# Fused attention and two FFNs in one planned program: other lead times and a later-transfer assumption in the planner, constants by one GpSimd transfer, twelve early vector operations on GpSimd

## The chip, the cores and the metric

The kernel runs on one core of one Trainium2 chip. The metric is the device time of one execution in microseconds (us); the time quoted is the median of three runs. "Before" is the kernel as it stood, 839.82 us.

## The reference, cut to what matters

```python
def _attn_ref(q, k, v):                 # q, k, v: [4, 8, 576, 64]
    scores = (1 / sqrt(64)) * q @ k^T
    mask = (rel >= 0) & (rel < 64)      # rel = query position - key position
    scores = where(mask, scores, -1e9)
    attn = exp(scores - max)
    attn = attn / (sum(attn) + 1e-9)
    return attn @ v

x = attention as [2304 tokens, 512]
x = square(relu(x @ moe_w_in)) @ moe_w_out        # 512 -> 2048 -> 512
out = leaky_relu(x @ moe2_w_in, 0.01) @ moe2_w_out
```

The FFN weights arrive as 64-bit floats and are turned into 32-bit words on the chip.

## The kernel before, in words

The 2304 tokens are cut into 18 blocks of 128. Attention is windowed, so a block of queries sees 192 keys. Each block has two quads of four heads. A quad is: scores on PE (`scores`, L495), mask with scale on DVE (`mask`, L516, one operand in PSUM, the other the mask tile), row maximum on DVE (L530), four exponentials on ACT (L533), sum and reciprocal on DVE (L541, L542), normalisation on DVE (`norm` in `softmax`, L545, two operands in SBUF), transpose on PE against an identity tile (L565), copy on ACT, product with v on PE (`weigh`, L574), and a split of the result into a rounded part (ACT, L366) and a remainder (DVE, L369). The split serves all large products: each is done as three fp32r products, high by high, high by low and low by high.

A weight chunk of w_in or w_out of the first FFN (`weight`, L425) is loaded as 64-bit words (L390, three buffers `wst`), rebiased on ACT (L399), put together by three DVE operations (L402, L408, L414), cast on ACT (L366) and given its remainder on DVE (L369). Of the second FFN the weights are converted to DRAM (`weight_to_dram`, L442) while earlier stages run, and read back later.

In order of time the stages are: the first quads (blocks 0 and 1, then 2 to 5), the first FFN's units on tokens 0 to 767 (L730, `unit`; chunks j, and token parts A of 256, BB of 256, AB of 512 and C of 256), its second products (L742, `out_unit`), the third token group in plain steps while the remaining blocks of attention are computed, a "wide" stage for the last 1024 tokens with seven products for eight (L982, `wide_pair`), its second products (L742), then the second FFN with seven products for eight: first layer `pair` (L1104, from `x_combos` of the stored x and sums of weights) and second layer `superblock` (L1294).

What sets the order: nothing is ordered by hand. `build` records some thousand operations, each with engine, assumed cost, due time, reads, writes and buffers, into `Plan`. `Plan.order` (L164) then runs an event model with those costs: each engine takes the ready operation that is due first, a buffer is given out when its last user is done in the model, and a transfer takes an assumed issue time, start, rate and completion. The sequence that comes out is written into each engine's queue, in which the chip goes strictly in order. The table `PRM` (L46) holds the due times' lead values: `DS`, `SB`, `END` for the quads, `AL` and `CS` for the rebias and the DVE steps of a weight conversion, `EV0`, `EV1` for the evacuations at the end of a stage, `WP`, `W7` for the operand sums, `XS` for `x_combos`, `WI`, `WO2` for the stretch over which the second FFN's weights are converted. At the start, 40 products of zeros (`WARM`, L1420 to L1428) have the lowest priority of all: PE takes one whenever the model has nothing else ready for it. `NCOLD` of them are taken to be slower than the others.

The constants are three transfers at the start: a mask for pattern 1 on SP's queue (L509 called at L1430), a mask for pattern 0 (L1431) and the identity (L1432) on ACT's queue. Later pattern masks are loaded into the first tile's second half on SP's queue.

GpSimd (POOL) does nothing before but four memsets of constants.

Of the kernel before, what the change touches and what calls it, by code (L numbers as in the profile page):

```python
# [100 lines left out]
class Plan:  # L101
# [182 lines left out]
@with_exitstack  # L284
def attention_then_two_ffns(
    ctx: ExitStack,
    tc: tile.TileContext,
    qp: bass.AP,
    kp: bass.AP,
    vp: bass.AP,  # L290
    w1: list,
    w2: list,
    caps: bass.AP,
    ident: bass.AP,
    out: bass.AP,
):
    plan, _ = build(ctx, tc, qp, kp, vp, w1, w2, caps, ident, out)
# [8 lines left out]
def build(ctx, tc, qp, kp, vp, w1, w2, caps, ident, out, prm=PRM):  # L306
    nc = tc.nc
# [117 lines left out]
    def weight(k, c, gate=()):  # L425

        j, m = divmod(k, 2)
        cv = slot(ep, "e", [P, DM], I32, 4)
        w = slot(rings[f"w{m}"], f"w{m}", [P, 2, DM], F32R)
        wt[j, m] = w  # L430
        cs = prm["CS"]
        float_words(0, j, m, c, cv)
        op("act", act_cost(DM), c + 1.8 * cs, lambda: copy(w.ap[:, 0], f32(cv.ap)), [(cv, 0), *gate], [(w, 0)])
        op(
            "dve", dve_cost(DM), c + 2.5 * cs,
            lambda: sub(nc.vector, w.ap[:, 1], f32(cv.ap), w.ap[:, 0]),
            [(cv, 0), (w, 0)], [(w, 1)],
        )
# [66 lines left out]

    def load_cap(b, due, queue):

        dma(
            due, lambda: queue.dma_start(out=cap_s.ap[:, 1], in_=caps[:, pattern(b)]),  # L509
            P * P * 4, writes=[(cap_s, 1)],  # L510
        )

    def cap_of(b):
        return (cap_s, 1 if pattern(b) else 0)

    def mask(b, u, st):  # L516
        nc.vector.scalar_tensor_tensor(
            out=u.ap, in0=st.ap, scalar=SCALE,
            in1=cap_s.ap[:, cap_of(b)[1], :].unsqueeze(1).to_broadcast([P, HQ, P]),
            op0=ALU.mult, op1=ALU.min,  # L520
        )

    def softmax(u, dve_sum, due):

# [114 lines left out]
    def duo(b, e):  # L639

        if pattern(b):
            load_cap(b, e - prm["DS"] - 6.0, nc.sync)
# [27 lines left out]
        op("pe", 1.23, e - 1.8, run, rd, [(pv, 0)], margin=prm["SPARE"])  # L670
        to_x(b, pv, 0, KD, e - 0.6)
# [957 lines left out]
```

## Time and profile before

| | |
|---|---|
| runs | 839.82 us median (839.74 to 840.04) |
| profiled execution, its own time | 841.09 us |
| span of that execution, first to last instruction | 839.2 us |
| PE (matmul) | 819.8 us busy, 98% of the span |
| DVE | 584.1 us, 70% |
| ACT | 504.3 us, 60% |
| POOL | 0.2 us, 0% |

The profiled execution is 1.27 us above the median, and 1.89 us of its time lie outside the span. PE's share counts the products of zeros at the start and is a mean over all stages; which engine the others wait for changes from stage to stage, so the sections below go by stretches of the span.

### The profile page before, as it was taken

To read this page: it belongs to the slowest core of one execution; us is meant where nothing else is said; L and a number is where in the kernel's file an instruction comes from. 1 tells how busy PE (TensorE), PEld (TensorE's weight loads), DVE (VectorE), ACT (ScalarE), POOL (GpSimd) and SP (SyncE) were. 2 spreads that over 40 slices of the span, in tenths; PEclk is the share of its full clock that TensorE was granted. 3 is DMA by queue.
4 is the path that set the end of the run, shared out by engine and by line. 5 is a ranking of instruction groups with operands and counts; after the bars stand their busy time and mean duration, and the time that the engine had idled before them with its cause. 6 is when DMAs were issued, how large, how long until landed. Compare 5 with 4: busy or idle time off the path is not lost.

```text
span 839.2 us, 14312 instructions
## 1 busy us (share of the span) xinstructions
PE 819.8 (98%) x5312; PEld 739.6 (88%) x5312; DVE 584.1 (70%) x1000; ACT 504.3 (60%) x1094; POOL 0.2 (0%) x4
## 2 busy tenths in 40 slices
PE   9899999999999999999999989999999999999998
PEld 8788988888787888778888889999999999999998
DVE  5999289864555786777769897777764887555553
ACT  4889677665564657776446376565555876444441
POOL 0000000000000000000000000000000000000000
PEclk9999999999999999999999999999999999999999
DMA  8898345534311037778988789889866998766661
GB/s 288 273 305 276 111 138 178 169 105 132 113 58 52 1 121 242 251 231 297 326 285 301 242 259 345 301 297 325 294 225 246 390 415 300 250 207 226 207 207 57
DMA packets 90310, 189.82 MB, mean 226 GB/s; under 512 B 7808, under 2 KB 47488, under 8 KB 90240
## 3 DMA queue, kind: packets, MB, share of 16 engines
q1 hardware_dynamic: 89792, 188.38, 65.9%
q8 instruction: 42, 0.69, 0.4%
q10 hardware_dynamic: 448, 0.52, 0.3%
q14 instruction: 28, 0.23, 0.1%
HBM read 121.24 MB, written 67.63 MB: 225 GB/s over the span
## 4 chain that ended last, share of the span: by engine, by line
PE 72%; DMA 11%; DVE 8%; ACT 6%; issue 3%; SPq 0%; DVEq 0%; ACTq 0%
PE acc L742 16%; PE acc L1294 11%; PE h L730 8%; PE h L1104 6%; PE h L1294 5%; PE s L1104 4%; DMA wst<-w2b 3%; PE h L742 3%; PE s L1294 2%; DMA wst<-w1a 2%; PE h L982 2%; PE acc L1104 2%; PE t L1104 2%; PE t L1294 2%; PE t L982 2%
## 5 line engine op out<-in xcount | busy, mean ns | idle before, releaser
L742 PE MATMUL acc<-x,w 128*128 128x512 f32 x576 | 136.5, 392 | 0.1
L742 PEld LDWEIGHTS acc<-x,w 128*128 128x128 f32 x576 | 106.4, 188 | 22.6 <-issue 0.7
L730 PE MATMUL h<-x,w 128*128 128x512 f32 (+1 forms) x624 | 120.7, 345 | 1.2 <-ACT w L762 1.0
L730 PEld LDWEIGHTS h<-x,w 128*128 128x128 f32 x624 | 97.2, 189 | 15.7 <-ACT w L762 1.4
L1104 PE MATMUL h<-w,x 128*128 128x384 f32 x432 | 85.7, 336 | 4.5 <-ACT e L366 3.6
L1104 PEld LDWEIGHTS h<-w,x 128*128 128x128 f32 x432 | 75.6, 188 | 6.2 <-ACT e L366 4.9
L1294 PE MATMUL acc<-x,w 128*128 128x384 f32 x360 | 73.3, 334 | 0.0
L369 DVE TENSOR_TENSOR x<-m,x 128x768 fp32r<-128x768 f32 x50 | 47.1, 956 | 35.5 <-ACT x L366 35.4
L399 ACT ACTIVATE wst<-wst 128x512 f32<-128x512 f32 x64 | 43.1, 677 | 37.5 <-DMA wst<-w2b 17.2
L366 ACT CAST x<-m 128x768 fp32r<-128x768 f32 x50 | 41.4, 837 | 40.2 <-PE h L1294 18.7
L1294 PEld LDWEIGHTS acc<-x,w 128*128 128x128 f32 x360 | 63.4, 188 | 0.0
L1104 PE MATMUL s<-w,x 128*128 128x384 f32 x288 | 58.3, 336 | 2.4 <-DVE m L1128 1.3
L369 DVE TENSOR_TENSOR w<-m,w 128x768 fp32r<-128x768 f32 (+1 forms) x50 | 44.8, 905 | 17.8 <-ACT w L366 17.7
L366 ACT CAST w<-m 128x768 fp32r<-128x768 f32 (+1 forms) x50 | 39.4, 797 | 26.8 <-PE h L1294 10.8
L1104 PEld LDWEIGHTS s<-w,x 128*128 128x128 f32 x288 | 50.3, 188 | 3.8 <-DVE m L1128 1.9
L742 PE MATMUL acc<-g,w 128*128 128x512 f32 x192 | 49.4, 398 | 0.0
L369 DVE TENSOR_TENSOR x<-wst,x 128x512 fp32r<-128x512 f32 (+2 forms) x45 | 34.1, 775 | 18.9 <-ACT x L366 17.1
L408 DVE SCALAR_TENSOR_TENSOR e<-wst,e 128x512 int32<-128x512 int32 x64 | 43.9, 686 | 1.1
L414 DVE SCALAR_TENSOR_TENSOR e<-wst,e 128x512 int32<-128x512 int32 x64 | 43.8, 684 | 0.7
L881 DVE TENSOR_TENSOR wst<-wst 128x256 f32<-128x256 f32 x96 | 39.3, 419 | 5.5 <-DMA wst<-wq 4.6
L742 PEld LDWEIGHTS acc<-g,w 128*128 128x128 f32 x192 | 35.1, 188 | 7.6 <-issue 0.5
L366 ACT CAST x<-wst 128x512 fp32r<-128x512 f32 (+2 forms) x45 | 30.2, 690 | 16.0 <-DVE wst L881 9.0
(167 smaller groups left out, 1534.3 us busy)
## 6 DMA issues: line engine op xcount, KB each, us to landing
m<-gd SPq DMA_DIRECT2D x38, 768.0 KB, 4.5
wst<-wq SPq DMA_DIRECT2D x22, 512.0 KB, 6.7
gd<-g SPq DMA_DIRECT2D x26, 384.0 KB, 4.9
gd<-m SPq DMA_DIRECT2D x24, 384.0 KB, 4.3
gd<-wst SPq DMA_DIRECT2D x22, 384.0 KB, 4.2
wst<-w1a SPq DMA_DIRECT2D x16, 512.0 KB, 5.2
v<-vp SPq DMA_DIRECT2D x32, 256.0 KB, 3.6
wst<-w2a SPq DMA_DIRECT2D x16, 512.0 KB, 4.4
```

What stands on the lines that cost most here:

```text
L366: nc.scalar.copy(out=dst, in_=src)
L369: eng.tensor_tensor(out=lo, in0=src, in1=f32(hi), op=ALU.subtract)
L399: nc.scalar.activation(out=top, in_=top, func=AF.Copy, scale=2.0**-112)
L408: nc.vector.scalar_tensor_tensor(out=cv.ap, in0=words(1), scalar=-(1 << 31), in1=cv.ap, op0=ALU.bitwise_and, op1=ALU.bitwise_or,)
L414: nc.vector.scalar_tensor_tensor(out=cv.ap, in0=words(0), scalar=29, in1=cv.ap, op0=ALU.logical_shift_right, op1=ALU.bitwise_or,)
L730: nc.tensor.matmul(out=hp.ap, lhsT=wi[:, a, kk, :], rhs=x.ap[:, b, kk, c0 : c0 + n], start=(kk == 0 and m == 0), stop=(kk == KD - 1 and m ...
L742: nc.tensor.matmul(out=a, lhsT=w.ap[:, i, d * P : (d + 1) * P], rhs=g[:, b], start=first and m == 0, stop=last and m == 2, skip_group_chec ...
L881: lambda: nc.vector.tensor_tensor(out=cv.ap[:, k], in0=cv.ap[:, in0], in1=cv.ap[:, in1], op=how),
L982: nc.tensor.matmul(out=ps.ap, lhsT=wc.ap[:, v, k, i * P : (i + 1) * P], rhs=x.ap[:, u, i], start=begin and i == 0 and m == 0, stop=i == 1 ...
L1104: nc.tensor.matmul(out=ps.ap, lhsT=wc.ap[:, v, k, i * P : (i + 1) * P], rhs=x.ap[:, u, n], start=begin and i == 0 and m == 0, stop=i == 1 ...
L1294: nc.tensor.matmul(out=bank[into][i].ap, lhsT=w.ap[:, v, p, i * P : (i + 1) * P], rhs=u.ap[:, x, e, j], start=begin and n == 0 and j == 0 ...
```

## The change

1. The numbers in `PRM` are new. `AL` goes from 0.6 to -0.23 (the rebias falls due 0.83 later against its conversion), `CS` from 0.7 to 1.71, `SB` from 6 to 7.66, `DS` from 12 to 13.62, `WO2` from (-40, 90) to (-56.72, 88.93), `XS` from (24, 40) to (17.78, 27.52), `NCOLD` from 14 to 8. `WF0`, `WF1`, `XC` and `WO` are read nowhere in the code.
2. The model lets every transfer issued by SP that lands after 12 us land 0.83 us later (`SLACK`). A product of zeros is assumed to cost 0.44 or 0.225 us instead of 0.22 or 0.18, and some PE groups of attention some 0.1 us more.
3. Masks and identity come in one transfer of 192 KB, issued by GpSimd.
4. On GpSimd instead of DVE: `norm` of blocks 0 and 1 (four operations of 128x512, `NB`), and the remainder of the first eight weight chunks, four of w_in and four of w_out (`WB`).

```diff
 PRM = dict(
-    NDUO=4, NEARLY=2, DS=12.0, EXPC=0.5, SB=6, END=1.5, P0=5.2, LEAD=5.0, WF0=14.0, WF1=20.0, XC=18.0, WP=9.0, WO=8.0,
-    YP=1.0, FS=5.0, FMAX=1.3, EV0=0.5, EV1=1.5,
-    SPARE=0.2, NSUM=1, WARM=40, NCOLD=14, WC=0.18, WD=1e6, AL=0.6, CS=0.7,
-    QB=-0.5, QE=0.0, QC=0.0, QF=-8.0, QT=1, LA=4, LB=12, PA=2.5, PB=2.0, PAB=2.5, PC=1.5, NACC=6,
-    GA=0.1, QG=6.0, GS=5.0, LEAD2=8.0, XS=(24.0, 40.0),
-    E7=30.0, MC=2.0, W71=0.0, Q7=24.0, X7=9.0, W7=11.0, WI=(10.0, 30.0), WO2=(-40.0, 90.0),
+    NDUO=4, NEARLY=2, DS=13.62, EXPC=0.5, SB=7.66, END=1.96, P0=5.21, LEAD=5.0, WF0=14.0, WF1=18.56,
+    XC=24.53, WP=6.71, WO=9.71, YP=1.22, FS=5.0, FMAX=1.3, EV0=1.43, EV1=1.95, SPARE=0.22, NSUM=1, WARM=40,
+    NCOLD=8, WC=0.225, WD=1000000.0, AL=-0.23, CS=1.71, QB=-0.5, QE=-0.17, QC=0.7, QF=-6.16, QT=1, LA=4,
+    LB=12, PA=2.5, PB=2.0, PAB=2.5, PC=1.5, NACC=6, GA=-0.26, QG=6.0, GS=5.0, LEAD2=8.0, XS=(17.78, 27.52),
+    E7=30.0, MC=2.0, W71=0.0, Q7=23.81, X7=9.0, W7=8.98, WI=(11.03, 30.0), WO2=(-56.72, 88.93), NB=(0, 2),
+    WB=(0, 8), SLACK=0.83,
 )
...
+                    if eng == "sp" and end > 12.0:
+                        end += PRM["SLACK"]
...
+def pool_cost(n):
+    return 0.13 + n * 0.00247
...
-    cap_s = slot(const, "cap", [P, 2, P])
-    id_s = slot(const, "ident", [P, P])
-    idt = (id_s, 0)
+    con = slot(const, "con", [P, 3, P])
+    idt = (con, 2)
...
+        away = prm["WB"][0] <= k < prm["WB"][1]
         op(
-            "dve", dve_cost(DM), c + 2.5 * cs,
-            lambda: sub(nc.vector, w.ap[:, 1], f32(cv.ap), w.ap[:, 0]),
+            "pool" if away else "dve", pool_cost(DM) if away else dve_cost(DM), c + 2.5 * cs,
+            lambda: sub(nc.gpsimd if away else nc.vector, w.ap[:, 1], f32(cv.ap), w.ap[:, 0]),
...
+        away = prm["NB"][0] <= b < prm["NB"][1]
...
-            nc.vector.tensor_tensor(
+            (nc.gpsimd if away else nc.vector).tensor_tensor(
                 out=u.ap, in0=u.ap, in1=rc.ap.unsqueeze(2).to_broadcast([P, HQ, P]), op=ALU.mult
             )
...
-                "pe", 0.22 if i < prm["NCOLD"] else prm["WC"], prm["WD"],
+                "pe", 0.44 if i < prm["NCOLD"] else prm["WC"], prm["WD"],
...
-    load_cap(0, -99.95, nc.sync)
-    dma(-98.5, lambda: nc.scalar.dma_start(out=cap_s.ap[:, 0], in_=caps[:, 0]), P * P * 4, writes=[(cap_s, 0)])
-    dma(-99.4, lambda: nc.scalar.dma_start(out=id_s.ap, in_=ident), P * P * 4, writes=[idt])
+    op("pool", 4.4, -200.0, lambda: nc.gpsimd.dma_start(out=con.ap, in_=consts[:, 0:3]), (), [(con, i) for i in range(3)])
```

Where the order moves, at three places. PE's queue at the start of the program, before (`t<-w_111` are the products of zeros, `s` and `h` the score banks, `ident` and `con` the identity):

```order
L1424 MATMUL t<-w_111 128x128 x21
L501 MATMUL s<-w_117,w_113 64x128 x8
L501 MATMUL h<-w_117,w_113 64x128 x8
L1424 MATMUL t<-w_111 128x128 x5
L501 MATMUL s<-w_137,w_133 64x128 x8
L501 MATMUL h<-w_137,w_133 64x128 x8
L1424 MATMUL t<-w_111 128x128 x8
L565 MATMUL acc_248<-ident,w_176 128x128 x4
```

And the same place now:

```order
L1431 MATMUL t<-w_111 128x128 x12
L506 MATMUL s<-w_119,w_115 64x128 x8
L506 MATMUL h<-w_119,w_115 64x128 x8
L1431 MATMUL t<-w_111 128x128 x2
L506 MATMUL s<-w_128,w_125 64x128 x8
L506 MATMUL h<-w_128,w_125 64x128 x8
L1431 MATMUL t<-w_111 128x128 x6
L506 MATMUL s<-kr,qr 64x128 x8
L1431 MATMUL t<-w_111 128x128 x2
L572 MATMUL acc_256<-con,w_170 128x128 x4
```

Twelve products of zeros stand ahead of the first scores instead of 21, and block 2's scores (`kr,qr`) stand ahead of the first transpose. GpSimd's queue after its memsets, now (before, nothing stood there); `w_170` to `w_239` are the four quads of blocks 0 and 1, `w_365` to `w_531` the w_in chunks 0 to 3, `w_1391` on the w_out chunks:

```order
L1437 DMA con<-consts 128x384
L552 ISA
L552 TENSOR_TENSOR w_170<-w_170,rc 128x512
L552 TENSOR_TENSOR w_178<-w_178,rc 128x512
L552 TENSOR_TENSOR w_205<-w_205,rc 128x512
L552 TENSOR_TENSOR w_239<-w_239,rc 128x512
L374 TENSOR_TENSOR w_365<-e,w_365 128x512
L374 TENSOR_TENSOR w_420<-e,w_420 128x512
L374 TENSOR_TENSOR w_466<-e,w_466 128x512
L374 TENSOR_TENSOR w_531<-e,w_531 128x512
L374 TENSOR_TENSOR w_1391<-e,w_1391 128x512
```

[...] ACT's queue where `pair` begins, before (`wst` is the rebias of a w2b chunk, `e<-h` and `e<-s` the copies that free PE's banks):

```order
L366 COPY e<-s 128x384
L399 ACTIVATE wst<-wst 128x512
L366 CAST x_4850<-wst 128x1024
L366 COPY e<-h 128x384
L366 CAST w_4921<-m 128x384
L1135 ACTIVATE m<-m 128x384
L366 COPY e<-h 128x384
```

And now:

```order
L1142 ACTIVATE m<-m 128x384
L371 COPY e<-t 128x384
L371 COPY e<-h 128x384
L403 ACTIVATE wst<-wst 128x512
L1142 ACTIVATE m<-m 128x384
L371 CAST w_4943<-m 128x384
```

This rebias now stands behind all the first pair's copies; the rebias before it (not shown) stands ahead of the first of them.

## Rows read from the trace of the kernel before

**Rows 1.** Busy time by stretch: us, then PE, PEld, DVE, ACT, POOL, clock, DMA
```profile
9.70:28.50 18.80, 16.87 (x225) 14.53 (x220) 18.43 (x42) 15.80 (x58) 0.00 (x0) 1.00 0.86 305
28.50:40.00 11.50, 10.34 (x143) 8.91 (x141) 10.60 (x25) 9.97 (x33) 0.00 (x0) 1.00 0.84 278
40.00:60.00 20.00, 18.80 (x180) 16.23 (x177) 18.68 (x37) 16.76 (x46) 0.00 (x0) 1.00 0.94 296
60.00:80.00 20.00, 20.00 (x154) 16.41 (x153) 18.78 (x37) 17.60 (x43) 0.00 (x0) 1.00 0.85 270
80.00:114.00 34.00, 32.99 (x229) 30.53 (x228) 16.59 (x33) 24.83 (x69) 0.00 (x0) 1.00 0.39 135
114.00:320.00 206.00, 206.00 (x1649) 170.88 (x1649) 143.12 (x266) 120.83 (x331) 0.00 (x0) 1.00 0.35 112
320.00:470.00 150.00, 147.82 (x647) 120.53 (x646) 113.30 (x197) 92.77 (x161) 0.00 (x0) 1.00 0.80 273
470.00:500.00 30.00, 26.46 (x141) 24.32 (x140) 26.35 (x47) 17.94 (x35) 0.00 (x0) 1.00 0.77 260
500.00:600.00 100.00, 96.26 (x544) 93.67 (x543) 76.09 (x140) 60.10 (x128) 0.00 (x0) 1.00 0.92 314
600.00:839.20 239.20, 235.66 (x1358) 235.02 (x1356) 142.03 (x183) 126.40 (x195) 0.00 (x0) 1.00 0.70 249
```

**Rows 2.** Timeline of the start: start, us, engine, line, operation [idle before, releaser]
```profile
0.73 0.59 SPq L483 DMA_DIRECT2D w<-qp  x1
1.04 7.47 PEld L1424 LDWEIGHTS t<-w 128*128 128x128 f32 x42 [1.04 <-DVE w L1420]
1.38 0.82 SPq L509 DMA_DIRECT2D cap<-caps  x1
...
6.87 1.64 PEld L1424 LDWEIGHTS t<-w 128*128 128x128 f32 x14
...
8.63 0.76 PE L501 MATMUL s<-w,w 64*64 64x128 f32 x10
...
9.77 0.69 DVE L517 SCALAR_TENSOR_TENSOR w<-s,cap 128x512 f32<-128x512 f32 x1 [8.78 <-DMA qr<-qp]
```

**Rows 3.** DMA issues of the start: queue, count, KB each, us to landing
```profile
w<-kp ACTq DMA_DIRECT2D x2, 192.0 KB, 3.6
w<-kp SPq DMA_DIRECT2D x1, 384.0 KB, 5.5
w<-qp SPq DMA_DIRECT2D x2, 128.0 KB, 3.8
```

**Rows 4.** Timeline, DVE, around the fourth x remainder
```profile
27.07 0.40 DVE L402 TENSOR_SCALAR e<-wst 128x512 int32<-128x512 int32 x1
27.38 0.68 DVE L545 TENSOR_TENSOR u<-u,rc 128x512 f32<-128x512 f32 x1
27.99 0.42 DVE L369 TENSOR_TENSOR x<-acc,x 128x256 fp32r<-128x256 f32 x1
```

**Rows 5.** Timeline, PE, the first two FFN units
```profile
26.48 1.69 PE L730 MATMUL h<-x,w 128*128 128x256 f32 x12
28.12 0.66 PE L565 MATMUL acc<-ident,u 128*128 128x128 f32 x4
28.54 1.31 PE L730 MATMUL h<-x,w 128*128 128x256 f32 x9
29.78 0.73 PE L574 MATMUL acc<-u,v 128*64 128x64 f32 x16
30.44 0.62 PE L730 MATMUL h<-x,w 128*128 128x256 f32 x3
```

**Rows 6.** Waits: engine, line, waited for: us in total, times, longest
```profile
ACT wst L399 <- DMA wst<-w2b: 17.2, 9, 2.8
```

**Rows 7.** Timeline, PE, four of the waits from 470 us on
```profile
479.41 1.32 PE L1104 MATMUL s<-w,x 128*128 128x384 f32 x6 [1.16 <-ACT e L366]
...
484.12 1.33 PE L1104 MATMUL h<-w,x 128*128 128x384 f32 x6 [1.29 <-ACT e L366]
486.32 1.31 PE L1104 MATMUL h<-w,x 128*128 128x384 f32 x6 [0.88 <-ACT e L366]
...
576.57 2.37 PE L1104 MATMUL h<-w,x 128*128 128x384 f32 x12 [1.19 <-ACT e L366]
```

**Rows 8.** Timeline, ACT, two rebiases ahead of such copies
```profile
481.57 0.67 ACT L399 ACTIVATE wst<-wst 128x512 f32<-128x512 f32 x1 [2.21 <-DMA wst<-w2b]
...
575.50 0.65 ACT L399 ACTIVATE wst<-wst 128x512 f32<-128x512 f32 x1 [1.69 <-DMA wst<-w2b]
```

More of the change, by code (lines that the diff above doesn't have):

```diff
@@ L292, in attention_then_two_ffns @@
     w2: list,
-    caps: bass.AP,
-    ident: bass.AP,
+    consts: bass.AP,
     out: bass.AP,
 ):
-    plan, _ = build(ctx, tc, qp, kp, vp, w1, w2, caps, ident, out)
+    plan, _ = build(ctx, tc, qp, kp, vp, w1, w2, consts, out)
     order = plan.order()
@@ L303, in attention_then_two_ffns, with build @@
             fn()
-def build(ctx, tc, qp, kp, vp, w1, w2, caps, ident, out, prm=PRM):
+def build(ctx, tc, qp, kp, vp, w1, w2, consts, out, prm=PRM):
     nc = tc.nc
@@ L504, in scores, with load_cap @@
                     )
-    def load_cap(b, due, queue):
-        dma(
-            due, lambda: queue.dma_start(out=cap_s.ap[:, 1], in_=caps[:, pattern(b)]),
-            P * P * 4, writes=[(cap_s, 1)],
+    def load_cap(b, due):
+        src = 3 if pattern(b) == 2 else 0
+        dma(
+            due, lambda: nc.sync.dma_start(out=con.ap[:, 0], in_=consts[:, src]), P * P * 4, writes=[(con, 0)],
         )
     def cap_of(b):
-        return (cap_s, 1 if pattern(b) else 0)
+        return (con, 0 if pattern(b) else 1)
     def mask(b, u, st):
@@ L518, in mask, with softmax @@
             out=u.ap, in0=st.ap, scalar=SCALE,
-            in1=cap_s.ap[:, cap_of(b)[1], :].unsqueeze(1).to_broadcast([P, HQ, P]),
+            in1=con.ap[:, cap_of(b)[1], :].unsqueeze(1).to_broadcast([P, HQ, P]),
             op0=ALU.mult, op1=ALU.min,
         )
-    def softmax(u, dve_sum, due):
+    def softmax(b, u, dve_sum, due):
         nm = slot(sp, "nm", [P, HQ], F32, 3)
@@ L559, in softmax @@
             op("dve", 0.39, due[2], recip, [(sm, h) for h in range(HQ)], [(rc, 0)])
-        op("dve", dve_cost(512), due[2] + 0.2, norm, [(rc, 0), *ex], [(u, "n", h) for h in range(HQ)])
+        op("pool" if away else "dve", pool_cost(512) if away else dve_cost(512), due[2] + 0.2, norm, [(rc, 0), *ex], [(u, "n", h) for h in range(HQ)])
     def transpose(u, tp, pt, due):
@@ L564, in run @@
             for h in range(HQ):
-                nc.tensor.transpose(out=tp.ap[:, h, :], in_=u.ap[:, h, :], identity=id_s.ap)
-        op("pe", 0.36, due, run, [*((u, "n", h) for h in range(HQ)), idt], [(tp, 0)], margin=prm["SPARE"])
+                nc.tensor.transpose(out=tp.ap[:, h, :], in_=u.ap[:, h, :], identity=con.ap[:, 2])
+        op("pe", 0.44, due, run, [*((u, "n", h) for h in range(HQ)), idt], [(tp, 0)], margin=prm["SPARE"])
         op("act", act_cost(512), due + 0.4, lambda: copy(pt.ap, tp.ap), [(tp, 0)], [(pt, "t")])
@@ L633, in quad @@
         op("dve", dve_cost(512), e - 5.5 * f, lambda: mask(b, u, st), [(st, 0), cap_of(b)], [(u, 0)])
-        softmax(u, i < prm["NSUM"], (e - 4.7 * f, e - 4.0 * f, e - 2.4 * f))
+        softmax(b, u, i < prm["NSUM"], (e - 4.7 * f, e - 4.0 * f, e - 2.4 * f))
         transpose(u, tp, u, e + ay - 1.6)
@@ L641, in duo @@
         if pattern(b):
-            load_cap(b, e - prm["DS"] - 6.0, nc.sync)
+            load_cap(b, e - prm["DS"] - 6.0)
         vs = [load_v(b, c, False, e - 12.0) for c in range(2)]
@@ L647, in duo @@
         op(
-            "pe", 1.13, e - prm["DS"], lambda: scores(b, list(enumerate(sts))),
+            "pe", 1.24, e - prm["DS"], lambda: scores(b, list(enumerate(sts))),
             [(q, 0), (q, 1), (k, 0), (k, 1)], [(st, 0) for st in sts], margin=prm["SPARE"],
@@ L657, in duo @@
             d = 2.2 * c
-            softmax(us[c], False, (e - 9.8 + d, e - 9.0 + d, e - 6.4 + d))
+            softmax(b, us[c], False, (e - 9.8 + d, e - 9.0 + d, e - 6.4 + d))
         free = b < sum(BLOCKS[:NFIRST]) // P
@@ L669, in duo @@
         rd = [x for c in range(2) for x in ((us[c], "t"), (vs[c], 0))]
-        op("pe", 1.23, e - 1.8, run, rd, [(pv, 0)], margin=prm["SPARE"])
+        op("pe", 1.33, e - 1.8, run, rd, [(pv, 0)], margin=prm["SPARE"])
         to_x(b, pv, 0, KD, e - 0.6)
@@ L1608 @@
     caps = np.where(caps, 3.0e38, -1.0e9).astype(np.float32)
+    consts = np.stack([caps[:, 1], caps[:, 0], np.eye(P, dtype=np.float32), caps[:, 2]], axis=1)
     arrays = {
@@ L1612 @@
         "w1b": chunks(moe2_w_in), "w2b": bits(moe2_w_out),
-        "caps": caps, "ident": np.eye(P, dtype=np.float32),
+        "consts": consts,
     }
@@ L1624 @@
             tc, d["qp"], d["kp"], d["vp"], [d["w1a"], d["w1b"]], [d["w2a"], d["w2b"]],
-            d["caps"], d["ident"], o,
+            d["consts"], o,
         )
```

## The prediction, made before the change was run

> **What bounds the kernel now.** I read the busy time by stretch first, then the waits, then the timelines where a stretch loses time. In the stretches the reader should look for PE's missing microseconds, since almost all of the span is PE's work and no edit removes any of it but products of zeros. From 28.5 us on PE stands idle for 1.16, 1.20, 0, 1.01, 0, 2.18, 3.54, 3.74 and 3.54 us [rows 1], 16.4 us in all; the last 3.54 holds the program's tail, whose order hardly moves. From 114 to 320 PE has no gap. The start is another matter: up to the first FFN unit at 26.48 [rows 5] PE waits for a chain, and that chain is DVE's: 18.43 busy of 18.8 us, then 10.60 of 11.5, 18.68 of 20 and 18.78 of 20 [rows 1]. So three places can pay: what stands ahead of DVE's first mask, DVE's load up to 80 us, and the 9.46 us of gaps between 320 and 600.
>
> DVE's first mask begins at 9.77, and is put down to a transfer [rows 2]. I read it as PE's: the scores it reads began at 8.63, right behind 21 products of zeros (42 passes, 1.04 to 8.51) [rows 2], while their inputs, issued from 0.73 on with 3.6 to 3.8 us to landing [rows 2, 3], were there by about 6. The zeros were dearer than the plan took them for: 28 of their passes lie between 1.04 and 6.87, 0.208 each, and the last 14 take 1.64 us, 0.117 each [rows 2].
>
> **The change part by part.** The sum is made against the profiled execution, 841.09 us; the median is 1.27 lower.
>
> *Zeros ahead of the scores, 21 to 12.* 24 passes at 0.208 are 5.0 us: the scores can begin at 6.0 instead of 8.63. The second half of q no longer stands behind the mask's transfer on SP (0.82 of issue) [rows 2] and lands at 1.3 + 3.8 = 5.1 [rows 3]. From scores to mask it was 9.77 - 8.63 = 1.14 us [rows 2]; part of it now falls into the slow passes, so I take 1.4. First mask at 7.4, 2.4 earlier.
>
> *Constants on GpSimd's queue.* No row shows a transfer from that queue. The nearest take 3.6 and 5.5 us for 192 and 384 KB [rows 3]; from 0.8 on, the masks are there between 4.4 and 6.3, before 7.4. I cost it at nothing: PE's 24 passes and the scores hide it. Without that cover each late microsecond would be one of DVE's.
>
> *Four normalisations and four w_in remainders off DVE.* Behind another operation a 512-wide one costs DVE 0.61 us of its queue (27.38 to 27.99), the first conversion step 0.31 [rows 4]. From the first mask to the end of block 1's last x remainder DVE took 28.41 - 9.77 = 18.64 us. In the new order that stretch lacks four normalisations, two weight remainders, one L402 and one L408, and has one reciprocal pair more (0.3): 18.64 - 7 x 0.61 - 0.31 + 0.3 = 14.4. Left alone, DVE would end it at 7.4 + 14.4 = 21.8 instead of 28.41.
>
> It isn't left alone, since GpSimd's operations are on the path. No row shows one on 128x512. The lower bound is DVE's 0.68 for the same work [rows 4], the upper two such passes, 1.36, for an engine that fetches its two inputs one after the other; the plan in the diff reckons near the upper, which I take. Five stand in this stretch (four normalisations, one remainder). If none is waited for, x is ready at 21.8; if DVE waits out all five, at 21.8 + 5 x 1.36 = 28.6. I take half of each, 25.2.
>
> [...]
>
> PE gains less than x does. Before, it began at 26.48 on half products and ended its second unit at 31.06 [rows 5]. Now a unit starts on whole x (12 passes in one piece): 25.4, plus 24 passes (1.69 + 1.31 + 0.62, less overlap, some 2.9), two transposes and a v product (0.5, 0.5, 0.6) and a score group of 0.9 ends at 30.8. It has then done a transpose and a score group, 1.4 us, that stood behind 31.06 before. Net **-1.7** (bounds: x at 21.8 gives -5.1, at 28.6 gives +1.7).
>
> *28.5 to 114.* DVE, 95% busy up to 80 (66.5 of 70.3 us) [rows 1], loses the other remainders, and later ones come sooner; PE's gaps there are 1.16 + 1.20 + 1.01 = 3.37 [rows 1]. I take **-1.3**, 0.5 for each of the three remaining early operations less stops, bounds -2.5 and +0.5. The four w_out remainders fall where PE has no gap and DVE is busy 143 of 206 us [rows 1]: nothing, and that slack is the cover.
>
> *Later transfers in the plan.* ACT stood 17.2 us, nine times, at a rebias whose w2b chunk had not landed [rows 6], 1.9 each. Behind two of those stand copies that free PE's banks: the rebias at 481.57 waited 2.21, that at 575.50 waited 1.69 [rows 8], and PE's gaps of 1.29 and 1.19 follow; with 1.16 and 0.88 in the same place they are 4.52 us [rows 7]. Now the rebias falls due 0.83 later and its transfer is taken to land 0.83 later, together 1.66 of the mean 1.9, and the conversions of the second FFN's weights begin 16.7 us sooner, where DVE still has room. On ACT's queue one rebias now stands behind the first pair's copies, but one stands ahead of the first. So about half of 4.52, and a little lost elsewhere, since the whole order from 320 on is new: **-2.0**, bounds -4.5 (all four go) and +2.5 (two gaps like these arise).
>
> *`DS`, `SB`, `END`, `EV0`, `EV1` and the rest* move operations within stretches without gaps or are counted above; those read nowhere cost nothing.
>
> Sum: -1.7 - 1.3 - 2.0 = -5.0. 841.09 - 5.0 = 836.1 for a profiled execution, **834.8** against the median.
>
> **The rivals.**
>
> *The start's gain does not arrive (same).* If the mask comes late from GpSimd's queue (9.8 instead of 7.4), or the first multiplication does, DVE starts where it did. [...] In rows, the first multiplication would be wanted about 4 us after the first mask, near 11; a delay past that pushes all four, because they go in order, and 3.2 us of it take back what x gains (28.41 to 25.2). For it: no row shows that queue at work. [...]
>
> Time of this rival: no gain up to 114, and the middle's -2.0 halved, 839.82 - 1.0 = 838.8.
>
> [...]
>
> *More than forecast* is in the bounds: x at 21.8 and all four gaps gone, about 829.
>
> **How the numbers follow.** A measurement of this kernel can tell about 0.2% from no change, 1.7 us, so the edges are 838.1 and 841.5. Forecast case 0.66, all of it faster; no gain at the start 0.17, which I count as same; the stop 0.17, slower. The bounds added up give 827.7 and 844.5, and all at one end is unlikely; the range of 829.0 to 842.5 reaches to both rivals and leaves out the last part of each end. The forecast case by itself is 829.0 to 838.1.
>
> **What would show it.** The first mask near 7.4 and scores near 6.0; GpSimd multiplications of about 1.4 us between 11 and 20; the first unit's twelve passes near 25; DVE below 95% up to 80; in the waits, ACT on w2b well under 17.2; PE's idle from 470 to 600 under 7.28. [...]

## The result and the profile after

The changed kernel takes 829.85 us (median of 4 executions, 829.69 to 830.51; before, beside it, 839.93): ratio 0.9876, 95% interval 0.9859 to 0.9893. Its profiled execution took 829.81 us, with a span of 827.9 (before 839.2). The time lies inside the forecast's range and on the side that was forecast; but the gain, 10.1 us, is twice the 5.0 forecast.

I cut both spans at five places where the same product begins or ends. They are the first and last starts in these groups: the second products of the first FFN, the wide stage's first products, the pair stage's, the superblocks'. Before (operations by line: duration min/median/max in ns, then first and last start, us):

```profile
L742 PE MATMUL h<-x,w x192: 277/283/386, 113.6 to 196.8; 128*128 128x256 f32 x192
L982 PE MATMUL h<-w,x x126: 388/389/450, 314.8 to 387.3; 128*128 128x512 f32 x126
L1104 PE MATMUL s<-w,x x288: 331/334/444, 474.9 to 658.2; 128*128 128x384 f32 x144
L1294 PE MATMUL acc<-x,w x360: 334/334/334, 661.0 to 832.4; 128*128 128x384 f32 x180
```

After:

```profile
L749 PE MATMUL h<-x,w x192: 277/283/387, 108.6 to 193.5; 128*128 128x256 f32 x192
L989 PE MATMUL h<-w,x x126: 388/389/395, 311.6 to 382.3; 128*128 128x512 f32 x126
L1111 PE MATMUL s<-w,x x288: 333/334/446, 471.0 to 643.5; 128*128 128x384 f32 x144
L1301 PE MATMUL acc<-x,w x360: 334/334/334, 649.4 to 820.9; 128*128 128x384 f32 x180
```

| stage | before | after | gained |
|---|---|---|---|
| S: start to the first second product | 113.6 | 108.6 | 5.0 |
| A: to the last first product of the wide stage | 273.7 | 273.7 | 0.0 |
| B: to the first pair product | 87.6 | 88.7 | -1.1 |
| C: the pair stage, to the first superblock product | 186.1 | 178.4 | 7.7 |
| D: to the end of the span | 178.2 | 178.5 | -0.3 |

The sum is 11.3 us. A second traced execution of the changed kernel (`after_again`, below) has 4.0, -0.7, -1.7, 7.6 and -0.3, 8.9 in all; so S can differ by a microsecond between two executions of the same kernel, C hardly. The forecast had 3.0 for S, nothing for A and D, and 2.0 for what is B and C here. In the busy time by stretch, PE's idle time from 40 to 80 is gone, and from 470 to 600 it is 0.15 us where it was 7.28 [rows 1] (PE, PEld, DVE, ACT, POOL, clock, DMA):

```profile
40.00:60.00 20.00, 20.00 (x168) 17.33 (x167) 18.06 (x38) 17.63 (x55) 0.00 (x0) 1.00 0.94 322
60.00:80.00 20.00, 20.00 (x168) 17.11 (x168) 19.07 (x37) 17.88 (x43) 0.00 (x0) 1.00 0.88 288
470.00:500.00 30.00, 30.00 (x170) 28.95 (x169) 29.03 (x52) 21.83 (x43) 0.00 (x0) 1.00 0.91 312
500.00:600.00 100.00, 99.85 (x570) 98.46 (x569) 76.30 (x141) 62.85 (x131) 0.00 (x0) 1.00 0.92 312
```

The start, where [rows 2] stood: the zeros end at 5.9, the scores begin at 5.87, and the first mask at 7.01 waits for PE's scores, not for the constants. The first FFN unit begins at 23.70 instead of 26.48 [rows 5]. That overstates the gain: before, all 80 passes of the zeros were over by then, and now 18 of them, 2.7 us, still stand in PE's queue behind it.

```profile
1.06 4.88 PE L1431 MATMUL t<-w 128*128 128x128 f32 x24 [1.06 <-DVE w L1427]
5.87 0.98 PE L506 MATMUL s<-w,w 64*64 64x128 f32 x14
7.01 0.69 DVE L522 SCALAR_TENSOR_TENSOR w<-s,con 128x512 f32<-128x512 f32 x1 [6.01 <-PE s L506]
```

And the waits: ACT's on w2b, 17.2 us in nine [rows 6], are now

```profile
ACT wst L403 <- DMA wst<-w2b: 5.5, 5, 1.6
```

### The profile page after: what moved, and what is told of

Read it like the earlier page. It is cut to its first block, busy times and chain, and to the rows that moved or that the text cites. A ratio compares the mean times of both kernels' runs of the same rounds, so it can differ in the third digit from the quotient of the medians.

```text
span 827.9 us, 14352 instructions
## 1 busy us (share of the span) xinstructions
PE 816.9 (99%) x5312; PEld 739.4 (89%) x5312; DVE 582.6 (70%) x988; ACT 508.2 (61%) x1094; POOL 16.9 (2%) x17
## 4 chain that ended last, share of the span: by engine, by line
PE 78%; DVE 7%; DMA 5%; issue 5%; ACT 4%; POOL 0%; SPq 0%; DVEq 0%; POOLq 0%; ACTq 0%
PE acc L749 17%; PE acc L1301 12%; PE h L1111 9%; PE s L1111 6%; PE h L737 5%; PE h L1301 5%; PE acc L1111 3%; PE h L989 3%; PE t L1111 3%; PE s L1301 3%; PE h L749 2%; PE t L989 2%; PE t L1301 2%; PE t L581 2%; DMA wst<-w1a 1%
## 5 line engine op out<-in xcount | busy, mean ns | idle before, releaser
L749 PEld LDWEIGHTS acc<-x,w 128*128 128x128 f32 x576 | 106.3, 188 | 23.7 <-DVE e L799 1.4
L406 DVE TENSOR_SCALAR e<-wst 128x512 int32<-128x512 int32 x64 | 29.8, 466 | 27.4 <-POOL w L374 17.0
L412 DVE SCALAR_TENSOR_TENSOR e<-wst,e 128x512 int32<-128x512 int32 x64 | 45.0, 703 | 1.2
```

The source lines that it names most:

```text
L406: nc.vector.tensor_scalar(out=cv.ap, in0=words(1), scalar1=3, scalar2=0x7FFFFFF8, op0=ALU.logical_shift_left, op1=ALU.bitwise_and,)
L412: nc.vector.scalar_tensor_tensor(out=cv.ap, in0=words(1), scalar=-(1 << 31), in1=cv.ap, op0=ALU.bitwise_and, op1=ALU.bitwise_or,)
L749: nc.tensor.matmul(out=a, lhsT=w.ap[:, i, d * P : (d + 1) * P], rhs=g[:, b], start=first and m == 0, stop=last and m == 2, skip_group_chec ...
```

## The experiments

The theory after the result: the extra gain is C's, and a few numbers of the table made it. Candidates are SLACK (every transfer after 12 us is taken to land 0.83 us later), AL (the rebias falls due 0.83 us later), WO2 (the second FFN's w_out conversions begin 16.7 us earlier), and, as the rival, that any new order may hit or miss. All sixteen runs in one table; stages in us as above, "waits" are ACT's and DVE's waits on transfers within C, "gaps" PE's idle time there. Ratios are to the kernel before, run beside each on the same chip, with 95% intervals. There the executions scatter by some us, of the kernel before too (838.9 to 846.1 beside the first four), so ratios and stages are read, not the plain times. The stages come from one traced execution each. Two kernels were traced twice (changed and after_again, no_gpsimd_math and no_gpsimd_again): they differ from themselves by 1.0 and 2.1 us in S and by at most 0.8 in A, B and C.

| run | S | A | B | C | waits | gaps | D | span | ratio |
|---|---|---|---|---|---|---|---|---|---|
| before | 113.6 | 273.7 | 87.6 | 186.1 | 21.5 | 7.4 | 178.2 | 839.2 | 1 |
| changed | 108.6 | 273.7 | 88.7 | 178.4 | 3.0 | 1.3 | 178.5 | 827.9 | 0.9876 (0.9859-0.9893) |
| after_again | 109.6 | 274.4 | 89.3 | 178.5 | 5.5 | 1.3 | 178.5 | 830.3 | 0.9873 (0.9850-0.9897) |
| head_only | 114.1 | 276.5 | 88.3 | 185.8 | 21.6 | 7.0 | 178.4 | 843.1 | 1.0035 (1.0015-1.0054) |
| head_and_slack | 111.5 | 276.7 | 87.3 | 184.3 | 7.0 | 6.4 | 178.4 | 838.2 | 0.9963 (0.9936-0.9990) |
| head_and_wout2 | 113.7 | 276.1 | 93.1 | 185.5 | 13.3 | 7.1 | 178.4 | 846.8 | 1.0064 (1.0041-1.0087) |
| head_and_three | 110.9 | 275.4 | 88.7 | 178.9 | 5.2 | 2.0 | 178.4 | 832.3 | 0.9914 (0.9892-0.9935) |
| no_slack | 111.7 | 277.4 | 92.9 | 182.7 | 13.7 | 4.1 | 178.5 | 843.2 | 1.0042 (1.0016-1.0069) |
| no_al | 109.4 | 274.3 | 89.0 | 178.1 | 3.5 | 1.3 | 178.5 | 829.3 | 0.9862 (0.9837-0.9887) |
| no_late_transfers | 110.6 | 276.5 | 93.5 | 184.1 | 19.9 | 5.8 | 178.4 | 843.1 | 1.0050 (1.0028-1.0073) |
| no_early_wout2 | 108.8 | 274.3 | 87.2 | 188.4 | 4.8 | 8.6 | 178.4 | 837.1 | 0.9964 (0.9945-0.9983) |
| slack_0p6 | 109.3 | 277.0 | 89.4 | 180.7 | 8.4 | 2.7 | 178.4 | 834.8 | 0.9931 (0.9907-0.9954) |
| slack_1p05 | 111.0 | 275.0 | 88.5 | 182.8 | 3.0 | 4.0 | 179.9 | 837.2 | 0.9923 (0.9890-0.9955) |
| slack_1p4 | 109.3 | 272.6 | 87.3 | 183.2 | 7.0 | 4.9 | 182.2 | 834.6 | 0.9913 (0.9887-0.9940) |
| no_gpsimd_math | 108.8 | 271.5 | 87.9 | 177.9 | 3.8 | 1.3 | 178.5 | 824.6 | 0.9827 (0.9786-0.9868) |
| no_gpsimd_again | 110.9 | 272.3 | 88.5 | 178.7 | 4.4 | 1.3 | 178.5 | 828.9 | 0.9843 (0.9815-0.9870) |
| no_gpsimd_wout | 108.7 | 271.9 | 89.3 | 178.0 | 4.2 | 1.3 | 178.5 | 826.4 | 0.9852 (0.9829-0.9874) |
| zeros_back | 110.3 | 274.3 | 89.4 | 178.3 | 3.9 | 1.3 | 178.4 | 830.7 | 0.9885 (0.9858-0.9912) |

Every edit is to the table of numbers unless a line of code is shown; the head runs keep the changed kernel's code, also its dearer prices for some PE groups of attention. Where the table takes one line less, the lines of a run are one lower than the changed kernel's (L405 for L406).

### The head alone, and the two suspects undone

```diff
 head_only: the old table, and
+    NCOLD=8, WC=0.225, NB=(0, 2), WB=(0, 8), SLACK=0.0,
 no_late_transfers: the new table, and
-    AL=-0.23, SLACK=0.83,
+    AL=0.6, SLACK=0.0,
 no_early_wout2: the new table, and
-    WO2=(-56.72, 88.93),
+    WO2=(-40.0, 90.0),
 no_gpsimd_math: the new table, and
-    NB=(0, 2), WB=(0, 8),
+    NB=(0, 0), WB=(0, 0),
```

> The kernel with the head of the change alone: constants in one transfer from GpSimd, the dearer prices for the zeros (12 products of zeros ahead of the scores), four normalisations and eight weight remainders on GpSimd; SLACK is 0 and every other number of the table is the old one. If the change's gain lies in the middle's order (late transfers), this keeps only the head's part: the first mask near 7.0, the start of the second products about 3 to 5 us earlier than before, and the pair stage (first pair product to first superblock product) as long as before, 186 us, with its gaps near 7 us: about 836 us. If the pair stage gained only because everything in front of it came earlier, the gaps go here too and the time is about 830.

> The changed kernel with SLACK back at 0 and AL back at 0.6, all else as changed. If transfers that landed later than planned made the pair stage's gaps, they come back: pair stage 183 to 186 us instead of 178.4, ACT's waits at w2b rebiases 10 us or more, total 835 to 838. If the earlier start of the w_out conversions or another number did it, the pair stage stays near 178.4 and the total within 1.5 us of 829.9.

> The changed kernel with WO2 back at (-40, 90): the conversions of the second FFN's w_out begin 16.7 us later. If their earlier start took DVE's and ACT's load out of the pair stage, the gaps there come back and the time is 833 to 838; if late transfers were the cause, the time stays within 1.5 us of 829.9 with the pair stage near 178.4 us.

> The changed kernel with no arithmetic on GpSimd (NB and WB empty): twelve operations return to DVE, the constants still come from GpSimd's queue. If GpSimd's operations relieve DVE in the head although they stop it, the first FFN unit starts about 1 to 3 us later than in the changed kernel (23.7) and the time is 831 to 833. If the stops of DVE (some 3.4 us of lengthened DVE operations) eat what is saved (some 4.9 us), the time stays within 1 us of 829.9, and if they cost more than it, it falls below 829.

The head alone is slower than before, by 0.35%, a miss for every theory. Its first unit began at 24.8, 1.7 us sooner, and the second products at 114.1, later than before. So 2.2 us were lost in between. Gaps are not what grew: PE's from the first unit to the second products are 2.6 us, before 3.2. But 20 passes of zeros, 2.7 us, now stand behind the first unit, where before none did. The timelines of its ACT and PE show 16 of these passes and the longest of the gaps:

```profile
35.90 2.05 PE L1430 MATMUL t<-w 128*128 128x128 f32 x16
...
61.39 0.65 ACT L402 ACTIVATE wst<-wst 128x512 f32<-128x512 f32 x1 [3.35 <-DMA wst<-w1a]
...
62.33 0.57 ACT L768 ACTIVATE w<-h 128x512 f32<-128x512 f32 x1
...
62.96 6.09 PE L736 MATMUL h<-x,w 128*128 128x512 f32 x24 [1.29 <-ACT w L768]
```

A rebias waits 3.35 us for its w1a chunk, the activation that empties PE's bank stands behind it on ACT, and PE waits 1.29. So the first unit came earlier for the most part because zeros were put off, and the longest gap that is left stands behind weights that had not landed.

In the middle both suspects turned out to be needed. Without the later transfers the waits on transfers are back (19.9 of 21.5 us), C is 184.1, and A and B grow by 2.8 and 4.8 as well, so that the ratio is 1.0050, well above what was expected. Without WO2's earlier start the waits stay away (4.8), yet C is 188.4, longer than before. Its row and PE's waits in C:

```profile
470.30:658.70 188.40, 179.78 (x1010) 175.89 (x1010) 138.09 (x243) 116.14 (x236) 0.00 (x0) 0.99 0.85 292
...
PE acc L1110 <- ACT acc L370: 3.1, 4, 1.0
PE h L1110 <- ACT e L370: 3.1, 2, 1.8
PE s L1110 <- DVE m L1134: 1.8, 2, 1.2
PE t L1110 <- ACT t L370: 0.6, 1, 0.6
```

and the changed kernel's row for the same stage:

```profile
471.00:649.40 178.40, 176.98 (x1009) 174.41 (x1008) 132.06 (x233) 114.08 (x234) 0.00 (x0) 1.00 0.86 298
```

Ten more DVE operations (243 against 233) and 6 us more of DVE's time lie in C, and PE waits for ACT's copies and DVE's sums, not for transfers. That DVE's load makes these waits is read from the counts; some 1.7 us of C's 10 are a fall of the clock (last section). `no_gpsimd_math` is taken up below.

### Which of the numbers, and whether alone

```diff
 no_slack, no_al: the new table with SLACK=0.0; with AL=0.6
 head_and_three: head_only, and
+    SLACK=0.83, AL=-0.23, WO2=(-56.72, 88.93),
 head_and_slack, head_and_wout2: head_only with SLACK=0.83; with the new WO2
```

> The changed kernel with SLACK alone back at 0 (AL stays at -0.23). Both undone together gave a pair stage of 184.1 us instead of 178.4 and a span of 843.1 instead of 827.9. If the plan's later landing of every transfer is the part that counts, most of this comes back: pair stage 182 us or more, waits of DVE and ACT on transfers there 8 us or more, span above 836. If the later rebias (AL) is the part, the pair stage stays below 180 and the span within 3 us of 828.

> The changed kernel with AL alone back at 0.6, so that a rebias falls due 0.83 us sooner; SLACK stays. If only the later landing counts, the pair stage stays within 1 us of 178.4 and the span within 2 us of 828. If the later rebias counts, ACT's waits on w2b come back (8 us or more of 17) and the span is above 832.

> The old table of numbers with the head of the change (as in head_only) and three more of the change's numbers: SLACK 0.83, AL -0.23 and WO2 (-56.72, 88.93). If transfers in time and the conversions' earlier start are all that the middle needs, the pair stage falls from 185.8 us to below 180.5 and the span by 5 us or more against head_only, to 836 to 838. If the other numbers of the table are needed as well, the pair stage stays above 183 and the span above 840.

> The old table with the head of the change and SLACK 0.83 alone; AL and WO2 are old. Undoing WO2 alone left a pair stage of 188.4 us, undoing SLACK alone one of 182.7. If the two only work together, the pair stage stays at 184 us or more here, although the waits on transfers go; if SLACK does most by itself, it falls to 181 or less (178.9 with AL and WO2 besides).

> The old table with the head of the change and the new WO2 alone; SLACK is 0 and AL old. If the two only work together, the pair stage is 182 to 186 us; if the earlier conversions do most by themselves, 181 or less. The start of the second products stays near the 114.1 us of head_only in either case.

AL is out: C 178.1 and a ratio like the changed kernel's. SLACK carries the loss: 843.2 of span without it, 15.3 more than the changed kernel, and not in C alone: 3.1 in S, 3.7 in A, 4.2 in B, 4.3 in C. Three numbers on the old table bring C to 178.9, so the rest of the table isn't needed there. Neither number does it alone: SLACK takes 1.5 us from head_only's C, WO2 0.3, both (with AL) 6.9. The reading that fits is that each removes one of two limits. With SLACK alone, transfers are mostly in time (waits 7.0), but DVE has as much to do in C as before (135.8 us, against 132.1 in the changed kernel), and the gaps stay at 6.4. With WO2 alone DVE has room (131.5) but work waits for transfers (13.3); and the conversions it moved into B cost 4.8 us there (93.1 against 88.3), where with SLACK they cost 1.4 (88.7 against 87.3). Of the 4.8 some 3 are a fall of the clock behind PE's waits (last section). How a late transfer reaches PE there stands in no_slack's timelines of ACT, DVE and PE:

```profile
427.82 0.66 ACT L402 ACTIVATE wst<-wst 128x512 f32<-128x512 f32 x1 [5.39 <-DMA wst<-w2b]
...
428.51 0.43 DVE L405 TENSOR_SCALAR e<-wst 128x512 int32<-128x512 int32 x1 [5.26 <-ACT wst L402]
...
435.37 0.68 DVE L798 COPY e<-acc 128x512 f32<-128x512 f32 x1
...
436.11 4.55 PE L748 MATMUL acc<-x,w 128*128 128x512 f32 x12 [1.79 <-DVE e L798]
```

A rebias waits 5.39 us for its w2b chunk, DVE's conversion 5.26 for the rebias; DVE then works without a pause up to the copy of 435.37 that empties a bank, and PE has waited 1.79 for that bank.

SLACK pays in S too: 114.1 becomes 111.5 in the old table, and the changed kernel's 108.6 becomes 111.7 without it. Both steps are larger than S differs between executions, though not by much.

### How much SLACK

```diff
 slack_0p6, slack_1p05: the new table with SLACK=0.6; 1.05
 slack_1p4: no_gpsimd_math with SLACK=1.4
```

> The changed kernel with SLACK 0.6. If SLACK stands for a real lateness of transfers, the gain grows evenly with it: pair stage and span between those of SLACK 0 (182.7 and 843.2) and 0.83 (178.4 and 827.9), the pair stage at about 179.5. If any new order of the plan may hit or miss, the pair stage falls anywhere between 177 and 188 us.

> The changed kernel with SLACK 1.05. If SLACK stands for a real lateness of about 0.8 us, a quarter more costs little: pair stage within 1 us of 178.4 and span within 2 us of 828. If 0.83 was one lucky order, the pair stage is 181 us or more and the span above 831.

> The changed kernel without arithmetic on GpSimd and with SLACK 1.4 instead of 0.83. If 0.83 is about what transfers are late by, more buys nothing more: the pair stage stays within 1 us of 177.9, and the total lies within 2 us of the same kernel with 0.83 or above it. If transfers are still late at 0.83, the last gaps go too and the total falls by another 1 us or more.

Up to 0.83 the waits on transfers fall with each step, 13.7, 8.4, 3.0 us for 0, 0.6 and 0.83, and C with them: 182.7, 180.7, 178.4. They don't fall evenly: half of both falls comes with the last 0.23. Whether there is a lateness to count, the trace of before can tell, by its issues of the first and second FFN's weight chunks (median us to landing last):

```profile
wst<-w1a SPq DMA_DIRECT2D x16, 512.0 KB, 5.2
wst<-w2a SPq DMA_DIRECT2D x16, 512.0 KB, 4.4
wst<-w1b SPq DMA_DIRECT2D x16, 512.0 KB, 4.8
wst<-w2b SPq DMA_DIRECT2D x16, 512.0 KB, 5.1
```

The event model of that kernel, worked out from its code with its own queueing of transfers, has medians of 4.06, 3.91, 3.96 and 4.24 us for the same four groups. So the chunks did land 0.5 to 1.1 us later than planned, and 0.83 is in the middle of that. Not every transfer did: the 72 stores of 384 KB to `gd`, 4.84 in the model, have medians of 4.2 to 4.9.

At 1.05 the waits stay at 3.0 but C is 182.8 and the span 837.2, which is what had been set down beforehand for a lucky order at 0.83. That trace is of the slowest of its four executions (839.0, the others 834.6 to 835.6), and the intervals of the ratios (0.9923 against 0.9876) still touch. At 1.4, without GpSimd's arithmetic, the loss is clear: 834.7 us against 828.0. The rows of slack_1p05 around the largest gap (DVE, ACT, PE):

```profile
580.32 1.03 DVE L373 TENSOR_TENSOR x<-wst,x 128x512 fp32r<-128x512 f32 x2 [5.35 <-ACT x L370]
...
579.66 0.93 ACT L370 CAST x<-wst 128x512 fp32r<-128x512 f32 x2
...
582.66 0.49 ACT L1141 ACTIVATE m<-acc 128x384 f32<-128x384 f32 x1 [2.06 <-DVE wst L1194]
...
583.97 2.29 PE L1110 MATMUL acc<-w,x 128*128 128x384 f32 x6 [2.69 <-ACT acc L370]
```

DVE stands 5.35 us behind a cast that comes late in ACT's queue, and ACT then behind DVE, and PE behind ACT: no transfer is among the releasers. That too much SLACK makes the plan postpone what is in fact ready would explain it, but whether it is that, or one bad order among many, stays open: few values were run, one order each. So the lateness is real, and that 0.83 hits as well as it does may in part be luck.

### The arithmetic on GpSimd

```diff
 no_gpsimd_wout: the changed kernel, and
-        away = prm["WB"][0] <= k < prm["WB"][1]
+        away = prm["WB"][0] <= k < prm["WB"][1] and k % 2 == 0
 after_again: the changed kernel; no_gpsimd_again: no_gpsimd_math once more
```

> The changed kernel itself, so that the next three stand beside it on the same chip: span 828 us, pair stage 178.4, second products from 108.6.

> The changed kernel without arithmetic on GpSimd once more, beside the changed kernel itself: if the 3.3 us by which its span was shorter (824.6 against 827.9) are real, the same difference of 2.5 to 4 us shows here; if they were the chip's, under 1 us is left.

> The changed kernel with only the four w_out remainders (at 102 to 113 us, two of them 2.54 us long) back on DVE; the four normalisations and the four w_in remainders stay on GpSimd. If PE's gaps at 110.03 and 119.96 and the 1.7 us that the stretch from 108.6 to the wide stage lost come from the w_out remainders, both go: that stretch falls from 207.1 to 205.4 us and the span to 825 to 826.5. If they come from the early normalisations and w_in remainders, it stays at 207 and the span within 0.7 us of the changed kernel.

With GpSimd's four w_out remainders A is 273.7 and 274.4, and 274.3 in no_al; without them 271.9, 271.5 and 272.3, with the same products in it (1934 or 1935 records). So they cost some 2 us, although they were to lie under cover; the 0.0 of A in the result hides as much, gained and lost again. The changed kernel's POOL, DVE and PE timelines:

```profile
101.95 2.54 POOL L374 TENSOR_TENSOR w<-e,w 128x512 fp32r<-128x512 f32 x2 [68.51 <-ACT w L371]
...
103.28 1.49 DVE L406 TENSOR_SCALAR e<-wst 128x512 int32<-128x512 int32 x1 [15.83 <-POOL w L374]
...
110.03 0.98 PE L749 MATMUL h<-x,w 128*128 128x256 f32 x6 [0.46 <-ACT g L769]
...
119.96 0.33 PE L506 MATMUL t<-kh,qs 64*64 64x128 f32 x2 [0.56 <-DVE x L374]
```

DVE's next conversion, held up to 101.87 by ACT's cast from its buffer (101.27 + 0.60 on ACT's timeline), waits on until 103.28 for GpSimd's remainder, which reads that buffer too, and then takes 1.49 us beside the second remainder. Both gaps, 0.45 to 0.47 and 0.56 to 0.58 long, stand at the same place in the runs that keep these four on GpSimd (head_and_slack, no_al and zeros_back among them), and in none of the four without.

What the eight early operations are worth can't be told: the first unit begins at 24.2 without GpSimd's arithmetic and at 23.7 with it, 25.0 and 24.7 in the second pair, but with it 18 passes of zeros stand behind that unit and without it none. The kernels without the w_out remainders take 828.0 and 828.9 us where the changed kernel, beside them, takes 830.9. They are the best that ran; the intervals of their ratios still overlap with its own. The difference of 3.3 us in the spans of the first pair came as 1.4 in the second, between the two outcomes set down for it; by the medians of four it is 2.9.

### The zeros

```diff
 zeros_back: the new table with NCOLD=14, WC=0.18, and
-                "pe", 0.44 if i < prm["NCOLD"] else prm["WC"], prm["WD"],
+                "pe", 0.22 if i < prm["NCOLD"] else prm["WC"], prm["WD"],
```

> The changed kernel with the old prices for the products of zeros, so that 21 of them stand ahead of the first scores again instead of 12; constants, GpSimd and the rest of the table as changed. By the forecast's head term the first mask comes near 9.5 us instead of 7.0, the first FFN unit 2 to 2.5 us later than 23.7 and the second products later by as much, with all that follows: span 830 to 831. If DVE's later work sets the start of the second products whatever the first mask does (head_only gained 1.7 us at the first unit and lost it by 114), they start within 0.8 us of 108.6.

The first mask came at 8.50, the first unit at 25.0, the second products at 110.3, the span was 830.7. The changed kernel's two executions have their first mask at 7.01 and 7.99, the first unit at 23.7 and 24.7 and the second products at 108.6 and 109.6, the later ones on the same chip as zeros_back. So the earlier mask is worth 0.7 to 1.7 us at the second products, less than the 2 to 2.5 expected, and no more than S differs between executions by itself. The ratio's interval doesn't tell it from the changed kernel's.

## Where the prediction was right, and why it was wrong in size

**The step that failed** is the term *Later transfers in the plan*, -2.0 us, with -4.5 as its good bound. B and C gained 6.6 (5.9 in the second execution), beyond that bound. The direction and the place (work behind late transfers, 470 to 600) were right; the size was off in three ways.

First, it counted four gaps [rows 7], 4.52 us, and then half of them. C had ten, 7.4 us, of which 1.3 are left: also those put down to DVE's sums and to ACT's copies into `t` and `acc`. SLACK is on every transfer of the SP queue after 12 us, not on w2b's alone, and the waits on all of them in C fell from 21.5 to 3.0 (5.5 in the second execution). The rebias's later due time, which I gave half of the effect, has none that the runs show (no_al).

Second, a gap cost more than its length here. PE's busy time in C fell too, from 178.57 to 176.98, for the same 1009 products: 1.6 us with nine gaps fewer, 0.18 each. The other runs go the same way (178.89 with eleven gaps in head_only, 177.77 with five in head_and_slack).

Third, the earlier conversions stood in the step as a remark. They are half of the mechanism: without them C is 188.4, and without SLACK, in the old table, they cost 4.8 in B and bring 0.3 in C. Two limits lay one over the other, so each part alone looked worthless. That the change had a value of SLACK with no bad order in C was not foreseen by any step, and may be luck in part (slack_1p05).

**The head and the stretch to 114**, -3.0 forecast, came as -5.0 and, in a second execution, -4.0. Scores near 6.0 (5.87), mask near 7.4 (7.01), constants hidden, unit near 25 (23.7 and 24.7): right. But the cause was only partly the one given. The head alone brings nothing at 114 (head_only); SLACK, which the forecast had counted for the middle only, makes some 3 us of it, the zeros 0.7 to 1.7, GpSimd's arithmetic 0.2 to 1.3, the last two not clear of what S differs by itself.

**GpSimd's price.** 1.36 was taken, twice DVE's 0.68; how GpSimd fetches its inputs no run shows. Four normalisations took 1.03 to 1.33 and the early remainders 1.28 to 1.71. The half of each, 0.68, that I let DVE stand was somewhat too much: between 8 and 40 us DVE's operations took 3.8 us more than without GpSimd's arithmetic (1.0 in L412, 1.9 in L406, 0.6 in the normalisations that stayed, 0.4 in L546), 0.5 for each of GpSimd's eight. But I had forecast DVE under 95% up to 80; it is at 95% as before (66.6 of 70.3 us), and at 95% without GpSimd's arithmetic too (66.9), so this share could not show the relief. That the w_out remainders cost nothing was wrong: some 2 us, with a buffer that is freed later and a stop of 1.07 on DVE's next conversion.

**The rivals.** "The start's gain does not arrive" had the outcome of head_only right (1.0035) and its condition wrong: the mask is released by PE (7.01), and the first normalisation follows its reciprocal (11.17 + 0.18) at 11.50. What stands ahead of it in GpSimd's queue (the two `MODIFY_POOL_CONFIG` of L552) took 37 ns each and began at 1.9 and 2.0. What head_only gained at its first unit was for the most part zeros put off. That GpSimd stops DVE for its whole length, the stop of the forecast's slower case (0.17), is seen in single rows, below (1.65 us for an L412 that takes 0.68 alone), and not on the whole (3.8 us in eight operations). PE's granted clock stayed at 1.00 in every stretch of the changed kernel, taken as in [rows 1].

## What to carry to other kernels

Where a planner orders in-order queues, compare the landing times it assumes with the trace first: 0.83 us per transfer, counted for all of SP's after 12 us, was worth 4.9 us of span in the old table and 15.3 in the new, and the arithmetic moved to GpSimd was worth nothing that could be shown. Run the neighbours of a number that pays: 0.6 and 1.05 gave back a part of it. Where products of zeros fill a queue, count those that stand behind an earlier start before reading it as a gain. Look at two limits in the same stage together, since removing either alone may show nothing, or a loss. And of work moved to a slower engine (GpSimd took 1.03 to 1.71 us an operation up to 40 us, DVE 0.68 for the same) ask which buffer it holds, not only which engine it frees.

## What the runs showed of the hardware

**DVE and GpSimd stopped each other, also where DVE read one tensor.** The changed kernel's DVE and POOL timelines:

```profile
11.50 1.03 POOL L552 TENSOR_TENSOR w<-w,rc 128x512 f32<-128x512 f32 x1 [9.56 <-DVE rc L547]
12.95 1.04 POOL L552 TENSOR_TENSOR w<-w,rc 128x512 f32<-128x512 f32 x1 [0.41 <-DVE rc L547]
15.30 1.33 POOL L552 TENSOR_TENSOR w<-w,rc 128x512 f32<-128x512 f32 x1 [1.31 <-DVE rc L547]
24.80 1.45 POOL L374 TENSOR_TENSOR w<-e,w 128x512 fp32r<-128x512 f32 x1 [2.83 <-DVE pt L552]
...
13.29 0.98 DVE L406 TENSOR_SCALAR e<-wst 128x512 int32<-128x512 int32 x1
15.08 0.66 DVE L412 SCALAR_TENSOR_TENSOR e<-wst,e 128x512 int32<-128x512 int32 x1
16.25 0.41 DVE L546 TENSOR_SCALAR sm<-sm 128x4 f32<-128x4 f32 x1
25.14 1.65 DVE L412 SCALAR_TENSOR_TENSOR e<-wst,e 128x512 int32<-128x512 int32 x1
```

The L412 that begins inside the GpSimd operation of 24.80 takes 1.65 us and ends 0.54 after it. Where L412 came first (15.08), GpSimd's next one took 1.33 instead of 1.03. The L406, with one input, took 0.98 from 13.29, to 0.28 after GpSimd's end, and the small L546 of 16.25 took 0.41 instead of some 0.16. Over 8 to 40 us their means are (count, busy us, mean ns), in the changed kernel

```profile
L412 DVE SCALAR_TENSOR_TENSOR e<-wst,e 128x512 int32<-128x512 int32 x6 | 5.1, 844 | 0.1
L406 DVE TENSOR_SCALAR e<-wst 128x512 int32<-128x512 int32 x6 | 4.4, 725 | 0.0
```

and without arithmetic on GpSimd

```profile
L411 DVE SCALAR_TENSOR_TENSOR e<-wst,e 128x512 int32<-128x512 int32 x6 | 4.1, 676 | 0.0
...
L405 DVE TENSOR_SCALAR e<-wst 128x512 int32<-128x512 int32 x6 | 2.4, 417 | 0.0
```

So beside GpSimd the first conversion step (L406, one input) took 0.72 us in the mean and alone 0.42, the second (L412, two inputs) 0.84 and alone 0.68, both of 512 columns. What lengthens them is not shown. The masks and row maxima were not lengthened (0.66 to 0.69).

**Behind some of PE's waits its granted clock fell as well.** In no_slack PE stood 0.54 and 1.79 us within 3 us, and the granted clock then fell from 1.00 to 0.50 for some 3.4 us; twelve passes took 4.55 us (the row of 436.11 above), where the 36 ahead of these waits had taken 8.32, 2.77 for twelve. Busy time by microsecond:

```profile
435.00:436.00 1.00, 0.00 (x0) 0.00 (x0) 1.00 (x2) 0.00 (x0) 0.00 (x0) 1.00 1.03 374
436.00:437.00 1.00, 0.89 (x2) 0.80 (x3) 0.24 (x2) 0.89 (x2) 0.00 (x0) 0.51 1.11 413
...
438.00:439.00 1.00, 1.00 (x4) 0.81 (x3) 1.00 (x2) 0.00 (x0) 0.00 (x0) 0.50 1.01 393
439.00:440.00 1.00, 1.00 (x5) 0.82 (x4) 0.29 (x1) 0.00 (x0) 0.00 (x0) 0.78 0.99 373
```

At 0.50, 3.4 us lose 1.7 us of work, against 2.33 us of waits. The clock fell in head_and_wout2 (0.61 and 0.71 in the 5 us from 435 and from 440; at 0.50 that is some 7 us), no_late_transfers (0.83 in each of the same two), no_early_wout2 (0.85 and 0.81 from 480 and from 485), slack_1p05 (0.50 from 584 to 587) and slack_1p4 (0.66 in the 5 us from 580) too, each time behind a cluster of waits or a long one (2.69 us in slack_1p05). It is one reason why these are as slow as they are. The kernel before had 1.16, 1.29 and 0.88 us between 478 and 487 [rows 7] and kept 1.00.
